# State space scan and maxout FFN on one core: where VectorE's scan steps stand among the Strassen products

## The chip, the core and the metric

One core of a Trainium2 chip runs the whole program: TensorE (PE) multiplies matrices, VectorE (DVE) and ScalarE (ACT) work element by element, GpSimd (POOL) too, and SyncE (SP) issues most transfers. Matrix results land in PSUM, eight banks of 512 float32 values on each of 128 partitions; the rest lies in SBUF. Each engine works through its instructions in the order in which the program lists them. The metric is the time of one execution on the device in microseconds (us), as the median of several runs.

## The reference

For each of 4 batches and 8 heads, over 768 tokens, a state space scan (chunks of 32 in the reference), and then a feed-forward layer on the heads side by side:

```python
y_intra = (C B^T * exp(cum_i - cum_j) * causal) x          # cum: running sum of log a
y_inter = exp(cum_i) * (C state)
state   = exp(sum log a) * state + sum_j exp(cum_last - cum_j) B_j x_j
h   = maximum(maximum(y @ w1, y @ w2), y @ w3)             # y: 3072 x 256, w: 256 x 768
out = h @ w_out                                            # 768 x 256
```

Everything is float32 in and out; head dimension 32, state dimension 16.

## The kernel before

The 768 tokens are cut into six blocks of 128, numbered 0 to 5; one block holds 128 tokens of all four batches, 512 columns. Block 0 is done first, with plain matmuls for the three weight matrices (`up`, line 559 of the new text, 554 of the old). Blocks 1 to 5 use Strassen's scheme with seven products instead of eight: for each of the three weight matrices and three pairs of column tiles there is one step k, 0 to 8, which the text below calls "product k" of its block. `early(c, k)` issues four matmuls, two into the bank `sumA` and two into `sumB`; ScalarE copies the first (`eu`, line 639), VectorE adds up `eu`, `v` and an early sum (lines 640 to 642). `late(c, k)` then adds three more matmuls onto the same banks, so TensorE must wait there until the early readings are done. VectorE reads the results in lines 655 and 656 and takes the maximum over the three weight matrices (lines 655 and 660). `sumA` has one bank, `sumB` two, `ffn` one; four banks, `att`, serve the scan in turn.

While block c goes through its nine products, the scan of block n = c + 1 is prepared between them. In product 0 the inputs B and C are transposed (`trB`, `trC`), ScalarE scales C (`CT`) and takes exp of E, and VectorE makes the scaled C, `Cd` (line 435), by reading the bank of `trC`. In products 1 and 3 `scores` issues eight matmuls each (line 476), into four `att` banks; of each four, the last one takes the bank that `trC`, or the fourth bank of the first four, held. VectorE multiplies each of the four banks by its decays, in place (`scan_weight`, line 484). In products 5 to 7 the output y of the scan is summed up (lines 501 and 514) and copied (line 522). `scan_sums` makes four differences of y (line 532), which the Strassen products of the next block use. `down_next` issues one half of an output tile of the projection (line 676) for an earlier block, as work for TensorE between the early and the late matmuls or behind them; the last half of a tile is copied and stored (line 682). A float32 matmul stands in the trace as two records.

The order on each engine is that in which the code emits instructions; nothing reorders it but this: VectorE's scan steps and the maximum are not emitted on the spot but put into the list `later`, and `pop(n)` emits the first n of them. Where the `pop` calls stand thus sets VectorE's order. The names k, c and n are those of the last loop.

Of the kernel before, what the change touches and what calls it, by code (L numbers as in the profile page):

```python
# [13 lines left out]
ALU = mybir.AluOpType  # L14
# [5 lines left out]
def kernel(  # L20
# [20 lines left out]
    nc = tc.nc  # L41
# [4 lines left out]
    NC = S // P  # L46
# [52 lines left out]
    a0 = const.tile([P, P], FP32, name="a0")  # L99
    for k in range(REP):  # L100
# [5 lines left out]
        out=a_sb,  # L106
# [15 lines left out]
    def load(c, name):  # L122
        src, w = sources[name]
        t = blocks[c][name] = raw.tile([P, BH, w], FP32, tag="raw_" + name, name="raw_" + name)
        nc.sync.dma_start(
            out=t, in_=src[:, :, c * P:(c + 1) * P, :].rearrange("b h s n -> s (b h) n"))
# [74 lines left out]
    def decode():  # L201
# [21 lines left out]
        out=pick, in_=ident.rearrange("p (r k) -> p k r", k=BH), op=ALU.add, axis=AX.X)  # L223
    npick = const.tile([P, BH], FP32, name="npick")
    nc.vector.tensor_scalar(
        out=npick, in0=pick, scalar1=-1.0, scalar2=None, op0=ALU.mult)
# [4 lines left out]
        out=hsel, in_=hsel, pattern=[[-N, NH]], compare_op=ALU.is_ge, fill=0.0,  # L231
        base=0, channel_multiplier=1)
    nc.gpsimd.affine_select(
        out=hsel, in_=hsel, pattern=[[N, NH]], compare_op=ALU.is_ge, fill=0.0,
# [3 lines left out]
        out=parity, in_=hsel.rearrange("p (r g) -> p g r", g=2), op=ALU.add, axis=AX.X)  # L238
# [6 lines left out]
        out=mask, in_=mask, pattern=[[1, P]], compare_op=ALU.is_ge, fill=MASKED,  # L245
# [119 lines left out]
    def decay_load(c):  # L365
        L = decays(c)
        for b in range(0, NB, 2):
            nc.sync.dma_start(
                out=L[:, b:b + 2].rearrange("j b h i -> j (b h) i"),
                in_=cums[b * NH:(b + 2) * NH, c, :].partition_broadcast(P))  # L370

    def last_load(c):
        E = blocks[c]["E"] = raw.tile([HN, NB, P], FP32, tag="E", name="E")
        rows = cums[:, c].rearrange("(b h) s -> h b s", h=NH)
        for h in range(NH):
            nc.sync.dma_start(out=E[h * N:(h + 1) * N], in_=rows[h].partition_broadcast(N))
# [41 lines left out]
    def scan_c(c):  # L418

        st = blocks[c]  # L420
        tr = st["trC"]
        st["CT"] = CT = att.tile([HN, NB, 2, P], FP32, tag="CT", name="CT")
        for g in range(2):
            nc.scalar.mul(CT[:, :, g], tr, parity[:, g:g + 1])

    def scan_e(c):
        E = blocks[c]["E"]
        nc.scalar.activation(E, E, AF.Exp)

    def scan_cd(c):  # L430

        st = blocks[c]
        E = st["E"]
        st["Cd"] = Cd = att.tile([HN, NB, P], FP32, tag="Cd", name="Cd")
        nc.vector.tensor_tensor(out=Cd, in0=st["trC"], in1=E, op=ALU.mult)
# [86 lines left out]
            nc.scalar.copy(out=yT[c][:, t], in_=blocks[c]["y"][t].rearrange("p b i -> p (b i)"))  # L522

    def scan_sums(c):
        y11, y12, y21, y22 = (
            yT[c][:, k, r * HB:(r + 1) * HB] for k in range(2) for r in range(2))
        late = [blocks[c]["y"][k].rearrange("p b i -> p (b i)")[:, r * HB:(r + 1) * HB]
                for k in range(2) for r in range(2)]
        t = ysum[c % 2]
        for k, (a1, a0) in enumerate((  # L530
                (late[1], y11), (late[3], t[:, 0]), (late[3], y12), (late[2], t[:, 1]))):
            nc.vector.tensor_tensor(out=t[:, k], in0=a1, in1=a0, op=ALU.subtract)  # L532
        sides[c] = {1: y11, 2: y21, 3: y22, 4: t[:, 3], 5: t[:, 0], 6: t[:, 1], 7: t[:, 2]}


# [7 lines left out]
    def h_of(c):  # L543
        if c not in hT:
            hT[c] = ffn.tile([P, NF, BLK], FP32, tag="h", name="h")
        return hT[c]
# [31 lines left out]
    NW = 3 * NQ  # L578
# [16 lines left out]
    def weight_sums(k):  # L595
        q, i = divmod(k, 3)
        a11, a12, a21, a22 = (
            w_sb[i][:, kk, (2 * q + g) * P:(2 * q + g + 1) * P]
            for g in range(2) for kk in range(2))
        s1, s2, s3, s4 = (wsum[k][:, j] for j in range(4))  # L600
        nc.gpsimd.tensor_tensor(out=s1, in0=a21, in1=a22, op=ALU.add)
        nc.gpsimd.tensor_tensor(out=s3, in0=a11, in1=a21, op=ALU.subtract)
        nc.gpsimd.tensor_tensor(out=s2, in0=s1, in1=a11, op=ALU.subtract)
        nc.gpsimd.tensor_tensor(out=s4, in0=a12, in1=s2, op=ALU.subtract)
# [9 lines left out]
    def products(c, k, which, first):  # L614
        for p, bank, half in which:
            nc.tensor.matmul(  # L616
                out=bank[:, half], lhsT=left(p, k), rhs=sides[c][p],
                start=(first and half == 0), stop=True, skip_group_check=True)

    later = []  # L620

    def pop(n):
        while n and later:
            later.pop(0)()
            n -= 1
# [19 lines left out]
    def late(c, k):  # L645
        q, i = divmod(k, 3)
        m = held["m"]
        A, B, eu, t = held.pop("open")
        products(c, k, [(2, A, 0), (3, B, 0), (4, B, 1)], False)
        to = h_of(c)[:, 2 * q:2 * q + 2].rearrange(  # L650
            "p g (r t) -> p (g r) t", r=2) if i == 2 else m
        if i == 0:
            nc.scalar.copy(out=m[:, 0], in_=A[:, 0])
        else:
            nc.vector.tensor_tensor(out=to[:, 0], in0=m[:, 0], in1=A[:, 0], op=ALU.max)
        nc.vector.tensor_tensor(  # L656
            out=t[:, 0:2], in0=B, in1=eu[:, 1:2].to_broadcast([P, 2, HB]), op=ALU.add)
        pop(1)
        if i > 0:
            later.insert(0, lambda: nc.vector.tensor_tensor(  # L660
                out=to[:, 1:4], in0=m[:, 1:4], in1=t, op=ALU.max))

    downs = []

    def down_next(kind=ffn_bank):

        if not downs:
            return
        c, j = downs.pop(0)
        u, i, half = j // 4, j // 2 % 2, j % 2  # L670
        if j % 4 == 0:
            held["o"] = kind([P, 2, DM], "o")
        o = held["o"]
        b = 2 * u + i
        for f in range(half * NQ, (half + 1) * NQ):
            nc.tensor.matmul(  # L676
                out=o[:, i], lhsT=hT[c][:, f, b * P:(b + 1) * P], rhs=wo_sb[:, f],
                start=(f == 0), stop=(f == NF - 1), skip_group_check=True)
        if j % 4 == 3:
            ob = ffn.tile([P, 2, DM], FP32, tag="ob", bufs=3, name="ob")  # L680
            nc.scalar.copy(out=ob, in_=o)
            nc.sync.dma_start(
                out=out.rearrange("(b s) m -> s b m", s=S)[c * P:(c + 1) * P, 2 * u:2 * u + 2],
                in_=ob)
# [34 lines left out]
    for _ in range(6):  # L719
# [4 lines left out]
        out=cums.rearrange("k c s -> (k c) s").rearrange("(w r) s -> r w s", w=2), in_=a_sb)  # L724
# [31 lines left out]
    def loads(c):  # L756
        if c < NC:
            decay_load(c)
            last_load(c)
            load(c, "B")  # L760
            load(c, "C")
            load(c, "x")
# [41 lines left out]
    scan_y(1)  # L804
    part(2)
    scan_sums(1)
    weight_sums(1)
    down_next()

    for c in range(1, NC):  # L810
        n = c + 1
        for k in range(NW):
            early(c, k)
            if k < 4:
                for _ in range((1, 2, 1, 1)[k] if c == 1 else min(k, 1)):
                    part(n)
            else:
                part(n + 1)
            pop(2)

            if n < NC and k in (0, 1, 3, 7):
                if k == 0:
                    transposed(n)
                elif k == 7:
                    scan_own(n, (2, 3))
                    scan_y(n)
                else:
                    scores(n, k - 1)
            elif n < NC or k < NW - 1:
                if c > 1 or k % 2 == 0:  # L830
                    down_next()
            late(c, k)

            if c == 1 and k + 2 < NW:
                weight_sums(k + 2)
            if n < NC:
                if k == 0:
                    loads(c + 2)
                    scan_c(n)
                    scan_e(n)  # L840
                    later.append(lambda: scan_cd(n))
                if k < 3 and c > 1:
                    down_next()
                elif k == 3 and n + 1 < NC:
                    decay_mask(n + 1, 0)
                elif k == 4 and n < NC - 1:
                    scan_state(n)
                elif k == 5:
                    scan_old(n)
                elif k == 6:  # L850
                    pop(9)
                    scan_own(n, (0, 1))
                elif k == 7:
                    scan_sums(n)
        pop(9)
        while downs:
            down_next()
        downs += [(c, j) for j in range(8)]
    while downs:
        down_next(att_bank)  # L860
# [30 lines left out]
```

## Time and profile before

| | us |
|---|---|
| median of 3 runs | 335.22 (333.2, 335.22, 335.3) |
| profiled execution | 333.45 |
| its span, first to last instruction | 331.7 |
| TensorE busy in it | 302.5 |
| VectorE busy in it | 200.4 |
| ScalarE busy in it | 120.2 |

The span is what the rows tell of; the execution's own time holds 1.75 us around it. Busy times of different engines overlap. Where a row ends in brackets, the first number is how long the engine was idle before it, and the name behind the arrow is what ended that idle time. Times in the rows are counted from the span's start.

### The profile page before, as it was taken

Reading aid. Unit: us, or ns where it says so; the run is one execution under the profiler, and the core shown is the slowest. Engines: PE = TensorE matmul, PEld = TensorE weight load, DVE = VectorE, ACT = ScalarE, POOL = GpSimd, SP = SyncE. Lnnn points to the kernel's source line nnn. Section 1 sums busy time; section 2 is a strip of 40 time slices with the busy share of each in tenths; the row PEclk is TensorE's granted clock in tenths of the full one; section 3 lists DMA queues with packets and bytes.
Section 4 is the critical chain, followed back from the end, with each engine's and each line's share of the span. In section 5 each row is a group of like instructions: output and inputs, shape, how many; then the busy total and the mean of one; then the engine's idle time right before and its main releaser. Section 6 shows DMA issues by size and latency. Waiting matters only on the chain.

```text
span 331.7 us, 5268 instructions
## 1 busy us (share of the span) xinstructions
PE 302.5 (91%) x2016; PEld 228.0 (69%) x2016; DVE 200.4 (60%) x384; ACT 120.2 (36%) x311; POOL 72.5 (22%) x94
## 2 busy tenths in 40 slices
PE   6779998898889988979999879999897999999995
PEld 4534443586666865858887667877686777888874
DVE  2697656824847584736656484658366658466540
ACT  2847468467321524222354232244431021110200
POOL 5133573699105610000600100500000000000000
PEclk9999999999979999978999997999999999999999
DMA  8997989987910198500007890001000000010001
GB/s 87 273 355 197 146 246 252 126 160 217 120 13 0 34 239 112 65 32 2 0 2 209 141 126 0 3 1 34 0 2 31 0 2 32 0 35 0 32 2 63
DMA packets 105017, 28.13 MB, mean 85 GB/s; under 512 B 75296, under 2 KB 101920, under 8 KB 104992
## 3 DMA queue, kind: packets, MB, share of 16 engines
q1 hardware_dynamic: 104688, 27.66, 40.6%
q8 instruction: 16, 0.26, 0.3%
q10 hardware_dynamic: 304, 0.13, 0.1%
q14 instruction: 9, 0.07, 0.1%
HBM read 24.54 MB, written 3.24 MB: 84 GB/s over the span
## 4 chain that ended last, share of the span: by engine, by line
PE 66%; DVE 18%; ACT 7%; issue 4%; POOL 3%; DVEq 0%; ACTq 0%; POOLq 0%
PE sumB L616 19%; PE o L676 17%; PE sumA L616 17%; PE s L476 3%; PE y L514 3%; ACT L L390 3%; DVE L L484 2%; DVE v L641 2%; DVE eu L640 2%; DVE rb L532 2%; PE y L501 2%; POOL w_u L185 1%; DVE h L660 1%; DVE rb L656 1%; DVE w_u L176 1%
## 5 line engine op out<-in xcount | busy, mean ns | idle before, releaser
L676 PE MATMUL o<-wo,h 128*128 128x256 f32 x288 | 69.4, 381 | 1.3 <-DVE wo L188 1.3
L676 PEld LDWEIGHTS o<-wo,h 128*128 128x128 f32 x288 | 54.3, 190 | 9.9 <-DVE wo L188 2.1
L616 PE MATMUL sumA<-yT,w 128*128 128x256 f32 x180 | 59.1, 411 | 1.6 <-DVE eu L640 0.9
L639 ACT COPY eu<-sumA 128x256 f32<-128x256 f32 x45 | 16.8, 373 | 119.6 <-PE sumA L616 101.1
L390 ACT ACTIVATE L<-L,ncums 128x128 f32<-128x128 f32 x160 | 50.9, 396 | 11.4 <-POOL L L379 11.4
L616 PE MATMUL sumB<-rb 128*128 128x256 f32 x180 | 46.5, 381 | 0.0
L640 DVE TENSOR_TENSOR eu<-sumA,eu 128x256 f32<-128x256 f32 x45 | 19.1, 424 | 38.4 <-ACT eu L639 38.4
L616 PEld LDWEIGHTS sumA<-yT,w 128*128 128x128 f32 x180 | 32.3, 196 | 14.4 <-issue 4.8
L616 PEld LDWEIGHTS sumB<-rb 128*128 128x128 f32 x180 | 34.7, 193 | 4.9
L476 PE MATMUL s<-CT,BT 32*128 32x256 f32 x192 | 21.4, 427 | 15.5 <-DVE L L484 7.7
L554 PE MATMUL up<-yT,w 128*128 128x512 f32 x72 | 32.3, 598 | 1.5 <-DVE w L188 1.5
L484 DVE TENSOR_TENSOR L<-s,L 128x512 f32<-128x512 f32 x48 | 31.3, 682 | 0.0
L616 PE MATMUL sumB<-yT,rb 128*128 128x256 f32 x90 | 29.0, 405 | 1.8 <-DVE rb L642 1.2
L379 POOL TENSOR_SCALAR_AFFINE_SELECT L<-L 128x1024 f32<-128x1024 f32 x20 | 23.6, 1188 | 28.2 <-DMA L<-cums 28.2
L476 PEld LDWEIGHTS s<-CT,BT 32*128 32x128 f32 x192 | 12.2, 188 | 24.2 <-DVE L L484 9.9
L616 PE MATMUL sumB<-rb,w 128*128 128x256 f32 x90 | 28.2, 396 | 0.0
L616 PE MATMUL sumA<-rb 128*128 128x256 f32 x90 | 27.5, 388 | 0.0
L656 DVE TENSOR_TENSOR m<-sumB,eu 128x512 f32<-128x512 f32 x15 | 10.4, 692 | 26.6 <-PE sumB L616 26.6
L554 PEld LDWEIGHTS up<-yT,w 128*128 128x128 f32 x72 | 13.2, 190 | 18.1 <-issue 12.6
L656 DVE TENSOR_TENSOR rb<-sumB,eu 128x512 f32<-128x512 f32 x30 | 20.7, 691 | 7.4 <-PE sumB L616 7.0
L185 POOL TENSOR_TENSOR w_u<-w_u,w_r 128x512 uint32<-128x512 uint32 x12 | 18.1, 1506 | 31.4 <-DVE w_u L179 30.3
L616 PEld LDWEIGHTS sumB<-yT,rb 128*128 128x128 f32 x90 | 17.1, 198 | 7.3 <-DVE rb L642 2.4
(93 smaller groups left out, 330.4 us busy)
## 6 DMA issues: line engine op xcount, KB each, us to landing
L<-cums SPq DMA_DIRECT2D x10, 1024.0 KB, 9.3
rb<-in_moe_w_dram SPq DMA_DIRECT2D x9, 512.0 KB, 8.6
raw_x<-in_x_dram SPq DMA_DIRECT2D x6, 512.0 KB, 7.6
out_dram<-ob SPq DMA_DIRECT2D x12, 256.0 KB, 2.1
raw_B<-in_B_dram SPq DMA_DIRECT2D x6, 256.0 KB, 4.2
raw_C<-in_C_dram SPq DMA_DIRECT2D x6, 256.0 KB, 6.4
rb<-in_moe_w_out_dram SPq DMA_DIRECT2D x3, 512.0 KB, 5.7
E<-cums SPq DMA_DIRECT2D x40, 32.0 KB, 4.0
```

Source lines behind the costliest of these rows:

```text
L185: nc.gpsimd.tensor_tensor(out=u, in0=u, in1=r, op=ALU.add)
L379: nc.gpsimd.affine_select(out=Ls[c][:, b], in_=Ls[c][:, b], pattern=[[0, NH], [1, P]], compare_op=ALU.is_ge, fill=MASKED, base=0, channel_ ...
L390: nc.scalar.activation(L[:, b, h], L[:, b, h], AF.Exp, bias=ncum[c][:, b * NH + h:b * NH + h + 1], scale=1.0)
L476: nc.tensor.matmul(out=banks[r][:, i].rearrange("j g i -> j (g i)"), lhsT=st["BT"][rows, b], rhs=st["CT"][rows, b].rearrange("p g i -> p ( ...
L484: nc.vector.tensor_tensor(out=M, in0=s, in1=M, op=ALU.mult)
L514: nc.tensor.matmul(out=st["y"][t][q * D:(q + 1) * D, b], lhsT=st["x"][:, b * NH + h], rhs=M[:, b, h], start=(c == 0 and b == 0), stop=True ...
L554: nc.tensor.matmul(out=p, lhsT=w_sb[i][:, k, f * P:(f + 1) * P], rhs=yT[c][:, k], start=(k == 0), stop=(k == KD - 1))
L616: nc.tensor.matmul(out=bank[:, half], lhsT=left(p, k), rhs=sides[c][p], start=(first and half == 0), stop=True, skip_group_check=True)
L639: nc.scalar.copy(out=eu[:, 0], in_=A[:, 0])
L640: nc.vector.tensor_tensor(out=eu[:, 1], in0=A[:, 1], in1=eu[:, 0], op=ALU.add)
L656: nc.vector.tensor_tensor(out=t[:, 0:2], in0=B, in1=eu[:, 1:2].to_broadcast([P, 2, HB]), op=ALU.add)
L676: nc.tensor.matmul(out=o[:, i], lhsT=hT[c][:, f, b * P:(b + 1) * P], rhs=wo_sb[:, f], start=(f == 0), stop=(f == NF - 1), skip_group_check ...
```

## The change

The change touches only when VectorE's steps are emitted, and the place of one piece of the projection.

- `scan_sums` emits only the first of the four differences of y at once and puts the other three at the head of `later`.
- `late` no longer emits a step of its own and returns the maximum to the caller, which puts it at the head of `later` behind another `pop`.
- In product 0 the loads, the scaling of C, exp of E come ahead of that `pop`, so that Cd is emitted at the end of product 0. In product 1 the `pop` takes two steps, and so two score weights.
- After the early part of product 8 four steps are emitted: the three differences and the maximum. The block's last maximum waits until the next block's product 0.
- In block 1 a piece of the projection stands in product 8 and not in product 4.

```diff
@@ scan_sums
-        for k, (a1, a0) in enumerate((
-                (late[1], y11), (late[3], t[:, 0]), (late[3], y12), (late[2], t[:, 1]))):
-            nc.vector.tensor_tensor(out=t[:, k], in0=a1, in1=a0, op=ALU.subtract)
+        steps = [
+            lambda k=k, a1=a1, a0=a0: nc.vector.tensor_tensor(
+                out=t[:, k], in0=a1, in1=a0, op=ALU.subtract)
+            for k, (a1, a0) in enumerate((
+                (late[1], y11), (late[3], t[:, 0]), (late[3], y12), (late[2], t[:, 1])))]
+        steps[0]()
+        later[:0] = steps[1:]
@@ late
-        pop(1)
         if i > 0:
-            later.insert(0, lambda: nc.vector.tensor_tensor(
-                out=to[:, 1:4], in0=m[:, 1:4], in1=t, op=ALU.max))
+            return [lambda: nc.vector.tensor_tensor(
+                out=to[:, 1:4], in0=m[:, 1:4], in1=t, op=ALU.max)]
+        return []
@@ the loop over blocks and products
     scan_sums(1)
+    pop(9)
     weight_sums(1)
...
-            pop(2)
+            pop(4 if k == NW - 1 else 2)
...
-                if c > 1 or k % 2 == 0:
+                if c > 1 or k in (2, 6, 8):
                     down_next()
-            late(c, k)
+            maximum = late(c, k)
 
             if c == 1 and k + 2 < NW:
                 weight_sums(k + 2)
+            if n < NC and k == 0:
+                loads(c + 2)
+                scan_c(n)
+                scan_e(n)
+                later.append(lambda: scan_cd(n))
+            pop(2 if k == 1 else 1)
+            later[:0] = maximum
             if n < NC:
-                if k == 0:
-                    loads(c + 2)
-                    scan_c(n)
-                    scan_e(n)
-                    later.append(lambda: scan_cd(n))
                 if k < 3 and c > 1:
                     down_next()
...
-        pop(9)
-        while downs:
-            down_next()
+        if n == NC:
+            pop(9)
         downs += [(c, j) for j in range(8)]
```

VectorE's order, block 1, from the end of product 0 into product 1; before:

```order
L656 TENSOR_TENSOR m<-sumB,eu 128x512
L640 TENSOR_TENSOR eu<-sumA,eu 128x256
L641 TENSOR_TENSOR v<-sumB,eu 128x256
L642 TENSOR_TENSOR rb<-sumB,v 128x256
L435 TENSOR_TENSOR Cd<-trC,E 128x512
L655 TENSOR_TENSOR m<-m,sumA 128x256
L656 TENSOR_TENSOR rb<-sumB,eu 128x512
L484 TENSOR_TENSOR L<-s,L 128x2x256
```

and now (lines 640 to 642, 655, 656 and 660 are 645 to 647, 660, 661 and 664 in the new text):

```order
L661 TENSOR_TENSOR m<-sumB,eu 128x512
L435 TENSOR_TENSOR Cd<-trC,E 128x512
L645 TENSOR_TENSOR eu<-sumA,eu 128x256
L646 TENSOR_TENSOR v<-sumB,eu 128x256
L647 TENSOR_TENSOR rb<-sumB,v 128x256
L660 TENSOR_TENSOR m<-m,sumA 128x256
L661 TENSOR_TENSOR rb<-sumB,eu 128x512
L484 TENSOR_TENSOR L<-s,L 128x2x256 x2
```

Cd moved ahead of the three early steps of product 1, and two score weights (`L<-s,L`) stand where one did. In product 3 of the same block, before:

```order
L640 TENSOR_TENSOR eu<-sumA,eu 128x256
L641 TENSOR_TENSOR v<-sumB,eu 128x256
L642 TENSOR_TENSOR m<-sumB,v 128x256
L660 TENSOR_TENSOR h<-m,rb 128x768
L484 TENSOR_TENSOR L<-s,L 128x2x256
L656 TENSOR_TENSOR m<-sumB,eu 128x512
```

and now:

```order
L645 TENSOR_TENSOR eu<-sumA,eu 128x256
L646 TENSOR_TENSOR v<-sumB,eu 128x256
L647 TENSOR_TENSOR m<-sumB,v 128x256
L664 TENSOR_TENSOR h<-m,rb 128x768
L661 TENSOR_TENSOR m<-sumB,eu 128x512
```

The fourth weight of the first four left product 3. At the end of a block, from the last step of product 7 through product 8, now:

```order
L661 TENSOR_TENSOR rb<-sumB,eu 128x512
L532 TENSOR_TENSOR rb<-y,yT 128x256
L645 TENSOR_TENSOR eu<-sumA,eu 128x256
L646 TENSOR_TENSOR v<-sumB,eu 128x256
L647 TENSOR_TENSOR rb<-sumB,v 128x256
L532 TENSOR_TENSOR rb<-y,rb 128x256
L532 TENSOR_TENSOR rb<-y,yT 128x256
L532 TENSOR_TENSOR rb<-y,rb 128x256
L664 TENSOR_TENSOR m<-m,rb 128x768
L660 TENSOR_TENSOR h<-m,sumA 128x256
```

Before, all four differences (line 532) stood in front of `eu`. The other blocks change in the same way. GpSimd's and SyncE's own orders stay as they were; TensorE's and ScalarE's change only by the moved piece of the projection and its copy.

## Rows read from the trace of the kernel before

**Rows 1.** Span and mean granted clock; busy us, share of the span, instructions.

```profile
core 0: 331.7 us, clock 0.979
...
PE 302.5 (91%) x2016; PEld 228.0 (69%) x2016; DVE 200.4 (60%) x384; ACT 120.2 (36%) x311; POOL 72.5 (22%) x94
```

**Rows 2.** TensorE's waits: line, releaser, us in total, times, longest.

```profile
PE s L476 <- DVE L L484: 7.7, 4, 1.9
PE s L476 <- DVE Cd L435: 4.9, 4, 1.3
```

**Rows 3.** Stretches: length, busy us by engine, granted clock (before the last two).

```profile
92.00:100.00 8.00, 7.43 (x32) 6.02 (x33) 3.43 (x7) 1.93 (x6) 0.00 (x0) 0.79 0.02 3
128.00:132.00 4.00, 2.81 (x22) 1.94 (x22) 1.91 (x4) 1.55 (x5) 0.00 (x0) 1.00 1.22 115
144.00:152.00 8.00, 6.89 (x22) 5.10 (x23) 2.35 (x4) 0.61 (x2) 0.00 (x0) 0.58 0.00 0
200.00:204.00 4.00, 4.00 (x12) 2.91 (x11) 0.57 (x1) 0.37 (x1) 0.00 (x0) 0.59 0.00 0
248.00:252.00 4.00, 2.08 (x20) 1.25 (x19) 2.74 (x5) 1.55 (x5) 0.00 (x0) 1.00 0.19 66
```

**Rows 4.** Timeline, block 3, products 0 and 1: start, length, engine, instruction.

```profile
181.04 0.64 ACT L428 ACTIVATE E<-E 128x512 f32<-128x512 f32 x1
...
183.15 0.42 DVE L640 TENSOR_TENSOR eu<-sumA,eu 128x256 f32<-128x256 f32 x1 [1.93 <-ACT eu L639]
...
184.14 0.42 DVE L642 TENSOR_TENSOR rb<-sumB,v 128x256 f32<-128x256 f32 x1
184.51 0.69 DVE L435 TENSOR_TENSOR Cd<-trC,E 128x512 f32<-128x512 f32 x1
...
185.35 1.10 PE L476 MATMUL s<-CT,BT 32*128 32x256 f32 x10 [1.20 <-DVE Cd L435]
...
186.91 0.59 PE L616 MATMUL sumB<-yT,rb 128*128 128x256 f32 x2
```

**Rows 5.** Timeline, block 3, products 2 and 3.

```profile
190.59 0.42 DVE L640 TENSOR_TENSOR eu<-sumA,eu 128x256 f32<-128x256 f32 x1 [1.33 <-ACT eu L639]
...
194.32 0.68 DVE L484 TENSOR_TENSOR L<-s,L 128x512 f32<-128x512 f32 x1
...
197.18 0.42 DVE L642 TENSOR_TENSOR m<-sumB,v 128x256 f32<-128x256 f32 x1
...
198.39 0.69 DVE L484 TENSOR_TENSOR L<-s,L 128x512 f32<-128x512 f32 x1
...
199.13 1.42 PE L476 MATMUL s<-CT,BT 32*128 32x256 f32 x10 [1.92 <-DVE L L484]
```

**Rows 6.** Timeline, block 3's start: product 8 of block 2, product 0 of block 3.

```profile
172.10 0.41 DVE L532 TENSOR_TENSOR rb<-y,yT 128x256 f32<-128x256 f32 x1
...
172.41 0.37 ACT L639 COPY eu<-sumA 128x256 f32<-128x256 f32 x1 [1.52 <-PE sumA L616]
...
176.28 0.30 PEld L616 LDWEIGHTS sumA<-yT,w 128*128 128x128 f32 x2 [0.47 <-DVE h L655]
```

**Rows 7.** Timeline, block 1, products 2 and 3.

```profile
84.75 0.42 DVE L640 TENSOR_TENSOR eu<-sumA,eu 128x256 f32<-128x256 f32 x1
...
88.02 0.70 PE L616 MATMUL sumA<-yT,w 128*128 128x256 f32 x2 [0.25 <-DVE h L655]
```

**Rows 8.** Costliest groups: the projection; busy us, mean ns, idle before.

```profile
L676 PE MATMUL o<-wo,h 128*128 128x256 f32 x288 | 69.4, 381 | 1.3 <-DVE wo L188 1.3
```

**Rows 9.** Timeline, block 1, product 4 and product 8.

```profile
99.22 0.42 DVE L642 TENSOR_TENSOR rb<-sumB,v 128x256 f32<-128x256 f32 x1
...
100.16 0.59 PE L616 MATMUL sumB<-yT,rb 128*128 128x256 f32 x2
...
119.61 0.70 PE L616 MATMUL sumA<-yT,w 128*128 128x256 f32 x2 [0.91 <-DVE eu L640]
```

**Rows 10.** Timeline of SyncE's queue, block 1.

```profile
115.59 0.37 SPq L368 DMA_DIRECT2D L<-cums  x1
```

## Prediction

> **What bounds the kernel now.** I read the share of each engine first, then who waits for whom on TensorE, then the granted clock by stretches, then the timeline at the places that the change touches. TensorE is busy 91% of the span and VectorE 60% [rows 1]: TensorE sets the time, and what can be won is its idle time and its lost clock. In its list of waits two lines stand out, both on the scores matmuls of line 476: 7.7 us in four waits of up to 1.9 us for the weighting of line 484, and 4.9 us in four waits of up to 1.3 us for Cd of line 435 [rows 2]. Both are VectorE work. The third loss is the clock. Its mean is 0.979 of 331.7 us [rows 1], so 7.0 us are lost, and 6.7 us of that lie in three stretches: 8 us at 0.79, 8 us at 0.58 and 4 us at 0.59, which lose 1.68, 3.36 and 1.64 us [rows 3]. At full clock TensorE runs at 2.4 GHz; in these stretches it runs in part at the other level, 1.2 GHz.
>
> The reader should see where the clock falls. Blocks 1, 2 and 3 each have one low stretch, and each follows the 1.92 us wait of product 3 (in block 3 the wait ends at 199.13 [rows 5] and the low window begins at 200). Block 4 has the same wait, TensorE busy only 2.08 us of 4 there, and keeps its clock [rows 3]. After the 1.2 us wait of product 1 the clock is full: the window 128:132 is one of four such places [rows 3]. So the longer wait brings the fall three times in four, the shorter one never.
>
> **Part 1: Cd in product 0.** Now VectorE does Cd behind eu, v and the last early sum of product 1, at 184.51, and the fourth scores bank, which the transposed C held until then, comes free at 185.2; TensorE goes on at 185.35 after 1.20 us [rows 4]. In the new order Cd stands ahead of eu. It waits for ScalarE's exp of E, which ends at 181.04 + 0.64 = 181.68. VectorE is idle for 1.93 us before eu at 183.15 [rows 4], so Cd's 0.69 us fit: it ends near 182.4, an estimate, and TensorE wants the bank at 185.35 - 1.20 = 184.15. What is queued behind the waiting Cd is eu, which waits longer anyway, for ScalarE's copy. What comes next on TensorE are the late products. Those in sumB stand at 186.91; they would start at 185.7 and need the early sum that ends at 184.14 + 0.42 = 184.56 [rows 4]. So nothing else is late, and the whole 4.9 us goes. Bounds: 0 if another reader holds the bank, 4.9.
>
> **Part 2: score weights in pairs.** Of the first four weightings, product 1 takes two and not one, and the fourth leaves product 3, where it ran at 198.39 and released TensorE at 199.13 [rows 5]. It now stands where the third stands, 194.32 + 0.68 = 195.0, over 1 us before the scores of product 3. The extra one in product 1 takes 0.68 us ahead of eu of product 2; there VectorE is idle for 1.33 us [rows 5], in blocks 2 to 4. Once the wait is gone the late products of product 3 come 1.92 us sooner and need the sum that ends at 197.60 [rows 5], long past by then. Gain 7.7 us; bounds 0 to 7.7.
> In block 1 there is no such cover: eu of product 2 follows the weighting at 84.75 with no idle time, and TensorE waits already 0.25 us for line 655 at 88.02 [rows 7]. There I count 0.6 us of cost, since neighbours on VectorE overlap a little (the sum that ends at 184.56 is followed by Cd at 184.51 [rows 4]); bounds 0 and 0.7.
>
> **Part 3: the clock.** Without the waits of product 3 I take the three low stretches as gone: 6.7 us; bounds 0 and 6.7, below nothing too if new gaps bring new falls (a rival). I take the upper end because the fall never follows the gaps of 1.2 us or less, and no wait as long as 1.9 us remains in these blocks. The Trainium skill (TensorE: Matmul & The Clock Gate, section HAM oscillation — how this bites in real kernels) shows the clock falling after waits on transfers between bursts of matmuls, and the waits in its example are longer than any here. By that rule the waits of product 3 would not be the cause, and the sum would be 321.9; the trace does not agree, since each of the three falls comes straight behind a wait of 1.92 us.
>
> **Part 4: the sums of y.** Three of the four go behind the last product's early sums, and the last maximum goes into the next block. What gates the next block is line 655 of product 8: it frees the only sumA bank, and TensorE waits 0.47 us for it at 176.28 [rows 6]. Ahead of line 655 stands the same VectorE work as before, only in another order, so this wait stays. The order adds a little: the first sum ends at 172.10 + 0.41 = 172.51, and behind it now comes eu, which must wait for ScalarE's copy to end at 172.41 + 0.37 = 172.78 [rows 6]. That is 0.27 us of idle time, less what the second sum no longer waits for the first; I take 0.2 us. Four boundaries: 0.8 us of cost; bounds 0 and 1.6. The deferred maximum lies in product 0 behind the early sums, where VectorE waits for TensorE's late products anyway; I cost it at nothing, and without that cover it would be its own length at each boundary.
>
> **Part 5: the projection moved in block 1**, from product 4 to product 8. In product 4 its cover goes: the late products in sumB, now at 100.16, could start sooner by its length (6 of 288 records that take 69.4 us: 1.45 us [rows 8]), but wait for the early sum that ends at 99.22 + 0.42 = 99.64 [rows 9], so only 0.4 us is won. In product 8 TensorE waits 0.91 us for eu and more behind it [rows 9]; the projection fills that and costs nothing, since line 655 still gates. Gain 0.4 us; bounds -1.0 (not hidden at all, 1.45 less 0.4) and 0.4. With it moves block 0's last store, and behind that in SyncE's queue stand the loads for block 4, issued from 115.59 on [rows 10]. They will go out some 5 us later, an estimate (the wait in product 8 ends at 119.61 [rows 9], and the projection and its copy follow), and are wanted a block later, so I cost that at nothing; without that cover it would be up to 5 us once.
>
> **Sum** against the profiled execution (333.45 us, span 331.7 [rows 1] and 1.75 around it): 333.45 - 4.9 - 7.7 - 6.7 + 0.6 + 0.8 - 0.4 = 315.2. The median of the runs is 335.22, that is 1.77 more, about one further low-clock stretch (block 1's costs 1.68), which would go with the others. So I give 315.2 for the median too; if the difference has another cause, 317.0.
>
> **Rivals.**
> - *The clock is not won back* (14%): the falls have another cause than the wait, since block 4 has the wait and no fall [rows 3], and the same three stretches turn up elsewhere. 315.2 + 6.7 = 321.9; with one or two short ones 316.9 to 318.5. Against it: no fall stands anywhere else in these blocks. The Trainium skill's example in part 3, with its longer waits, would speak for it.
> - *The wait of product 1 stays* (6%), since ScalarE's copies of the same bank or the exp of E release it later than I read: 315.2 + 4.9 = 320.1. Against it: both end at 181.68 or sooner.
> - *The wait of product 3 stays with its clock loss* (5%): the fourth weighting would wait on its decays and not on its turn: 315.2 + 7.7 + 6.7 = 329.6, a gain near what can just be told. Against it: the same weighting runs today with no idle time noted before it.
> - *VectorE's order is the bound, and it comes out slower* (5%): Cd (0.69), the extra weighting (0.68) and three sums (3 x 0.41) only delay eu, v and the early sum, and the late products wait for these in place of the waits removed. The waits and the clock loss stay, plus 4 x 2.6 us: 333.45 + 10.4 = 343.9. It decides where VectorE's idle time before eu is below 0.69 us in product 1 and 0.68 us in product 2. In blocks 2 to 4 these are 1.93 and 1.33 [rows 4, 5]; only block 1 is short [rows 7].
>
> **The numbers.** The forecast, 315.2, has 70%, with its own range 313 to 317.5 (the bounds of parts 4 and 5 and the 1.8 of the median). To hold 8 in 10 the range takes in most of the first two rivals: 312.8 to 321. About 1% is what a measurement of this kernel can tell from no change. Faster by more: the forecast, the first two rivals and some of the third, 92%; within 1%: 4%; slower: 4%.
>
> **What would show it.** Right: both lines of waits at line 476 are gone; Cd runs between the sum of product 0 and eu of product 1; scores stand as sixteen records in one run in products 1 and 3; the mean clock is 0.995 or more; block 4, at full clock already, shortens by 1.20 + 1.92 less 0.2, some 2.9 us; the wait for line 655 at the boundaries is 0.4 to 0.8 us. Wrong: a clock below 0.99, or TensorE waiting at line 616 for eu or the early sum by about what the scores waited.

## The result and the profile after

The changed kernel takes 308.87 us, the median of four runs (308.51 to 310.01), against 335.26 us before in the same comparison: a ratio of 0.922 with a 95% interval of 0.917 to 0.928. Run again beside the experiments it took 309.04 us, a ratio of 0.920 (0.917 to 0.922). The direction was right; 315.2 us was forecast with a range down to 312.8, so the gain was larger than the range allowed.

The span, clock and busy time of the changed kernel, in the columns of [rows 1]:

```profile
core 0: 306.7 us, clock 0.999
```

```profile
PE 287.5 (94%) x2016; PEld 220.6 (72%) x2016; DVE 199.5 (65%) x384; ACT 119.7 (39%) x311; POOL 72.4 (24%) x94
```

VectorE does the same work, 200.4 us before and 199.5 now; TensorE is busy 15.0 us less with as many instructions, and the lost clock went from 7.0 us to 0.3 us. TensorE's longest waits, in the columns of [rows 2]:

```profile
PE sumA L621 <- DVE h L660: 3.7, 5, 1.0
PE s L476 <- ACT CT L424: 2.9, 2, 1.5
PE spread L300 <- POOL mask L244: 2.5, 1, 2.5
```

Both lines of [rows 2] are gone; the two waits of line 476 that are left stand ahead of block 1. At the head is now the block boundary, line 660 (655 before). The timeline of block 3, which answers to [rows 4] and [rows 5]:

```profile
166.60 0.69 DVE L435 TENSOR_TENSOR Cd<-trC,E 128x512 f32<-128x512 f32 x1 [0.49 <-ACT E L428]
...
168.04 0.42 DVE L645 TENSOR_TENSOR eu<-sumA,eu 128x256 f32<-128x256 f32 x1 [0.75 <-ACT eu L644]
...
171.62 1.28 DVE L484 TENSOR_TENSOR L<-s,L 128x512 f32<-128x512 f32 x2
...
173.63 0.42 DVE L645 TENSOR_TENSOR eu<-sumA,eu 128x256 f32<-128x256 f32 x1 [0.73 <-ACT eu L644]
```

Cd ran in a gap in front of eu, and the pair of score weights in the gap in front of the next eu; VectorE still waits 0.75 and 0.73 us for ScalarE behind them, so in this block neither delayed anything.

Where the time went is seen from when each product starts on TensorE, that is, the distance from one `early` to the next. Before and after, in us, for the products that changed:

| product | block 1 | block 2 | block 3 | block 4 | sum of changes |
|---|---|---|---|---|---|
| 0 | 3.96, 3.97 | 5.81, 5.35 | 5.34, 5.35 | 5.35, 5.35 | -0.4 |
| 1 | 6.25, 4.62 | 7.44, 5.59 | 7.45, 5.59 | 7.44, 5.59 | -7.2 |
| 2 | 4.74, 5.25 | 5.61, 5.61 | 5.61, 5.61 | 5.61, 5.61 | +0.5 |
| 3 and 4 | 13.68, 9.10 | 15.23, 9.29 | 13.54, 9.29 | 11.42, 8.81 | -17.4 |
| 8 | 4.99, 5.17 | 4.99, 5.18 | 4.98, 5.46 | 4.98, 5.18 | +1.0 |

Products 5 to 7 and block 5 are as long as before, within 0.03 us each. The rest, 1.5 us, lies ahead of the blocks: block 1 starts at 73.07 before and at 71.53 here. In the second profile of the changed kernel it starts at 72.98, so that part is a difference between executions and not the change.

In block 1 product 1 won only 1.63 us. There Cd ends after the scores have started:

```profile
76.86 0.69 DVE L435 TENSOR_TENSOR Cd<-trC,E 128x512 f32<-128x512 f32 x1 [0.47 <-ACT E L428]
...
77.32 1.47 PE L476 MATMUL s<-CT,BT 32*128 32x256 f32 x16
...
78.72 0.70 PE L621 MATMUL sumA<-yT,w 128*128 128x256 f32 x2
```

The sixteen score records take 78.72 - 77.32 = 1.40 us to the next product, and 1.07 in the other blocks: a rest of the wait is left, 0.33 us, which the list does not show, since the records around it overlap it.

### The profile page after: what moved, and what is told of

Its sections match the earlier page's. It is cut to its first block, busy times and chain, and to the rows that moved or that the text cites. A ratio compares the mean times of both kernels' runs of the same rounds, so it can differ in the third digit from the quotient of the medians.

```text
span 306.7 us, 5262 instructions
## 1 busy us (share of the span) xinstructions
PE 287.5 (94%) x2016; PEld 220.6 (72%) x2016; DVE 199.5 (65%) x384; ACT 119.7 (39%) x311; POOL 72.4 (24%) x94
## 4 chain that ended last, share of the span: by engine, by line
PE 74%; DVE 13%; ACT 6%; POOL 3%; issue 3%; POOLq 0%; ACTq 0%; DVEq 0%
PE sumB L621 22%; PE sumA L621 20%; PE o L681 18%; PE y L514 3%; PE s L476 3%; ACT L L390 2%; DVE L L484 2%; PE up L559 2%; PE y L501 2%; POOL w_u L185 2%; DVE w_u L176 2%; DVE m L664 1%; DVE rb L532 1%; PE spread L316 1%; DVE v L646 1%
## 5 line engine op out<-in xcount | busy, mean ns | idle before, releaser
L621 PE MATMUL sumA<-yT,w 128*128 128x256 f32 x180 | 56.9, 398 | 4.0 <-DVE h L660 3.7
L621 PEld LDWEIGHTS sumA<-yT,w 128*128 128x128 f32 x180 | 31.1, 189 | 15.8 <-DVE h L660 5.7
L621 PE MATMUL sumB<-yT,rb 128*128 128x256 f32 x90 | 27.3, 385 | 1.0 <-DVE rb L647 1.0
L621 PE MATMUL sumA<-rb 128*128 128x256 f32 x90 | 26.8, 379 | 0.0
L621 PE MATMUL sumB<-rb,w 128*128 128x256 f32 x90 | 26.8, 379 | 0.0
L646 DVE TENSOR_TENSOR v<-sumB,eu 128x256 f32<-128x256 f32 x45 | 19.1, 425 | 4.7
L621 PEld LDWEIGHTS sumB<-yT,rb 128*128 128x128 f32 x90 | 16.4, 190 | 5.2 <-issue 2.0
L621 PEld LDWEIGHTS sumB<-rb,w 128*128 128x128 f32 x90 | 17.1, 190 | 2.3
L621 PEld LDWEIGHTS sumA<-rb 128*128 128x128 f32 x90 | 17.1, 190 | 2.4
```

What stands on the lines that cost most here:

```text
L621: nc.tensor.matmul(out=bank[:, half], lhsT=left(p, k), rhs=sides[c][p], start=(first and half == 0), stop=True, skip_group_check=True)
L646: nc.vector.tensor_tensor(out=v, in0=B[:, 1], in1=eu[:, 1], op=ALU.add)
```

## The wait was longer than its row

The forecast priced each wait of the scores by the idle time in the list. The rows of block 4, whose clock was full before and after, show what that misses. Before (start, length of the group, instructions):

```profile
248.83 0.71 PE L476 MATMUL s<-CT,BT 32*128 32x256 f32 x6
251.46 1.13 PE L476 MATMUL s<-CT,BT 32*128 32x256 f32 x10 [1.92 <-DVE L L484]
252.51 0.70 PE L616 MATMUL sumA<-yT,w 128*128 128x256 f32 x2
```

and the changed kernel, the same place:

```profile
226.24 1.15 PE L476 MATMUL s<-CT,BT 32*128 32x256 f32 x16
227.32 0.70 PE L621 MATMUL sumA<-yT,w 128*128 128x256 f32 x2
```

From the first score record to the next product it was 252.51 - 248.83 = 3.68 us, and is 227.32 - 226.24 = 1.08 us: the wait cost 2.60 us, not 1.92. The list counts idle time from the end of the row of six, 248.83 + 0.71 = 249.54. The other 0.68 us might be waiting that the list hides, or the cost of cutting a run of score matmuls in two. A run from the experiments below tells them apart. In it the same sixteen records are cut at the same place, but TensorE does other matmuls in between and never waits (block 3):

```profile
185.82 0.71 PE L478 MATMUL s<-CT,BT 32*128 32x256 f32 x6
186.46 2.86 PE L775 MATMUL o<-wo,h 128*128 128x256 f32 x12
189.24 1.12 PE L478 MATMUL s<-CT,BT 32*128 32x256 f32 x10
190.30 0.70 PE L618 MATMUL sumA<-yT,w 128*128 128x256 f32 x2
```

Six records take 186.46 - 185.82 = 0.64 us there and ten take 190.30 - 189.24 = 1.06, together 1.70, where sixteen in one run take 1.08. So 0.62 of the 0.68 us is the cost of the cut, with no waiting in it. The single records show how it comes about: a score matmul uses 32 of the 128 rows (`32*128`), and in the unbroken run four records at a time start within 0.02 us of each other, so sixteen records are four rounds. The six before the cut are two rounds of three, and the ten behind it are four rounds again: the matmul that was held back no longer runs beside its three neighbours. What is left is the row's end: the next matmul starts 0.64 us after the six begin, 0.07 us before the end that the trace gives them. For block 4 the wait thus is 1.92 + 0.07 us of idle time and 0.64 + 1.05 - 1.08 = 0.61 us for the cut, 2.60 in all. For product 1 of block 3 the same sum is 1.20 + 0.07 + (0.64 + 1.02 - 1.07) = 1.86, from [rows 4] and its neighbours:

```profile
183.44 0.71 PE L476 MATMUL s<-CT,BT 32*128 32x256 f32 x6
...
186.37 0.70 PE L616 MATMUL sumA<-yT,w 128*128 128x256 f32 x2
```

186.37 - 183.44 = 2.93 us against 1.07 now. The Trainium skill (Perfetto Trace Analysis, section Tensor Engine Instruction (MATMUL, LD_WEIGHTS)) says that TensorE's ends in a trace are computed and not observed. The trace agrees in that the next matmul starts before the given end, but only 0.07 us of the 0.68 lie there.

## Experiments

**Cd alone.** One line is added to the kernel before:

```diff
                     later.append(lambda: scan_cd(n))
+                    pop(1)
```

> The kernel before with Cd alone moved to the end of product 0; score weights, sums of y and the projection stay where they were. Theory (a wait costs what lies between the start of the scores and the start of the next products, less the 1.07 us that sixteen score records take in one run): product 1 shrinks by 1.6 to 1.86 us in each of blocks 1 to 4, 7.2 us in all. Rival (a wait costs the idle time that the list of waits shows): 4.9 us in all. Clock: if a fall follows the wait of product 3, which stays here, at least one low stretch remains right behind it, and the time is about 326 to 328 us; if the two waits of a block bring the fall only together, the clock is full and the time is near 321.

It took 322.32 us, a ratio of 0.964 (0.957 to 0.971). Product 1 went from 6.25, 7.44, 7.45 and 7.44 us to 4.63, 5.59, 5.59 and 5.59, 7.2 us in all; the size by starts is right and 4.9 is not. The waits of product 3 stood unchanged in the list:

```profile
PE s L476 <- DVE L L484: 7.7, 4, 1.9
```

The clock fell behind two of them, those of blocks 2 and 3 (columns as in [rows 3]; the waits end near 139 and at 189.5):

```profile
136.00:140.00 4.00, 2.08 (x19) 1.07 (x17) 2.74 (x5) 1.25 (x5) 0.00 (x0) 1.00 0.19 66
140.00:144.00 4.00, 4.00 (x11) 3.22 (x11) 0.93 (x2) 0.37 (x1) 0.00 (x0) 0.57 0.00 0
188.00:196.00 8.00, 6.47 (x27) 5.18 (x28) 3.57 (x7) 1.69 (x6) 0.00 (x0) 0.79 0.10 34
```

The time lies below the 326 to 328 us expected, because these two falls cost 1.72 and 1.68 us where before the three cost 6.7, and block 1 started 0.9 us earlier. So the place of the falls came as forecast here, and the time did not.

**Pairs alone.** The kernel before with

```diff
-        pop(1)
+        pop(2 if k == 1 else 1)
```

> The kernel before with two score weights in product 1 and the fourth in product 2, and nothing else; Cd stays in product 1, so its wait stays. Theory: product 3 shrinks at full clock from 6.9 us to 4.3 in each of four blocks, 10.4 us, product 2 of block 1 grows by 0.5, and the clock is full in all blocks, another 6.5: about 317 us. Rival on the size: 7.7 us and the clock, about 319.5. Rival on the clock (the fall does not hang on the wait of product 3): low stretches stay somewhere, about 323.5.

It took 316.37 us, 0.946 (0.938 to 0.954). Product 3 took 4.40, 4.30, 4.30 and 4.30 us, product 2 of block 1 went from 4.74 to 5.26, and every block kept full clock although the wait of product 1 stood as before:

```profile
PE s L476 <- DVE Cd L435: 4.9, 4, 1.3
```

So the clock's part hangs on the wait of product 3 and not on that of product 1, and the size by starts holds for it too: 333.45 - 10.4 - 6.7 + 0.5 = 316.9.

**The wait filled instead of removed.** To the kernel with Cd alone, in product 3 of blocks 2 to 4, between the third and the fourth score matmul:

```diff
+    def cover():
+        o = ffn_bank([P, 2, DM], "o")
+        for f in range(NF):
+            nc.tensor.matmul(
+                out=o[:, f % 2], lhsT=hT[n - 2][:, f, 0:P], rhs=wo_sb[:, f],
+                start=(f == 0), stop=(f == NF - 1), skip_group_check=True)
```

> The kernel with Cd alone moved, and in product 3 of blocks 2 to 4 six more matmuls of the projection's shape (2.6 us), whose sums nobody reads, issued between the third and the fourth score matmul, where TensorE otherwise waits for the score weight. The wait is not shortened, only filled. Theory (the idle time brings the fall): blocks 2 to 4 keep full clock behind product 3, product 3 takes the same 6.9 us as it did in block 4 at full clock, and the time is that of the kernel with Cd alone less the falls of blocks 2 and 3, some 5 us; block 1, not filled, may keep its fall. Rival (the place or the score matmuls bring the fall): falls in blocks 2 and 3 as before, the time no shorter.

It took 321.11 us, against 322.32 for the kernel without the filling; the two profiles' spans are 319.1 and 320.3. Both blocks kept full clock around product 3:

```profile
132.00:148.00 16.00, 16.00 (x110) 12.81 (x109) 10.92 (x21) 4.05 (x12) 0.00 (x0) 1.00 0.06 18
180.00:196.00 16.00, 16.00 (x82) 12.88 (x80) 10.85 (x21) 5.10 (x16) 0.00 (x0) 1.00 0.57 73
```

Product 3 took 7.7 us and not the 6.9 expected: the six matmuls take 189.24 - 186.46 = 2.78 us where the idle time was 1.99, and the cut in the scores costs as much as before. That eats 2.4 us, and only the two falls, 3.4 us, were there to win; so the 5 us expected were too many. For the cause it speaks plainly in one direction: in blocks 2 and 3 the clock fell in both profiles with the idle wait and in neither block with the wait filled. The mean clock of all their executions bears it out: 0.979 to 0.989 in the four with Cd alone, 0.997 to 0.999 in the four with the filling, 1.000 in the four with the pairs. It is not a proof for every wait, since blocks 1 (here and with Cd alone) and 4 have the idle wait and kept their clock; what decides between them the runs do not show.

**The boundary as it was.** The changed kernel with the four differences of y in one piece and the last maximum at the block's end:

```diff
-        steps[0]()
-        later[:0] = steps[1:]
+        for step in steps:
+            step()
...
-            pop(4 if k == NW - 1 else 2)
+            pop(2)
...
-        if n == NC:
-            pop(9)
+        pop(9)
```

> The changed kernel with the four differences of y in one piece behind product 7 again, and the block's last maximum at the block's end. Theory (the same VectorE work gates line 660 of the new text in either order, and the new order adds 0.2 us of idle time): product 8 goes from 5.2 us back to 5.0 in each of four blocks, and where GpSimd works beside the last maximum (block 1's end) product 0 of block 2 may grow by 0.4; 308 to 309 us, 0 to 0.8 shorter. Rival (the sums behind the early steps were worth something): 1 us or more longer.

308.45 us against 309.04 for the changed kernel beside it:

> The changed kernel once more, as the measure for the other kernels that run beside it: about 309 us, mean clock 0.995 or more, each block's products as in its first profile.

Product 8 took 4.98 to 4.99 us in all four blocks, against 5.17, 5.18, 5.45 and 5.18. So this part of the change costs 1.0 us by the traces; the medians differ by 0.6, within the spread of the runs. Product 0 of block 2 did not grow by the 0.4 us that I had allowed for; it took 5.36 us, as in the changed kernel.

**Line 660 first.** From [rows 6] and the wait at the head of the new list: what stands in front of line 660 in product 8 but is not needed yet goes behind it.

```diff
-            pop(4 if k == NW - 1 else 2)
+            pop(2)
...
-            later[:0] = maximum
+            if n < NC and k == NW - 1:
+                later.extend(maximum)
+            else:
+                later[:0] = maximum
```

> The changed kernel, but in product 8 only two of the three remaining differences of y go ahead of line 660's reading of sumA; the fourth comes behind it, and the maximum of product 7 waits for the next block's product 0 along with the last one. Theory (this reading gates the next block's first product; 0.34 + 0.87 us of VectorE work leaves its front, TensorE idles there 0.70 to 0.98 us): product 8 shrinks by 0.7 to 1.0 us in four blocks, 3 to 4 us in all, 305 to 306 us. Rival (the two maxima in product 0 delay its late readings and move the wait there): product 0 grows by as much, no gain.

It took 305.17 us, a ratio of 0.908 to the kernel before (0.906 to 0.910), 3.9 us below the changed kernel. Product 8 of block 2 in the changed kernel, and then in this one:

```profile
159.84 0.95 DVE L664 TENSOR_TENSOR m<-m,rb 128x768 f32<-128x768 f32 x1
...
160.71 0.41 DVE L660 TENSOR_TENSOR h<-m,sumA 128x256 f32<-128x256 f32 x1
...
161.17 0.70 PE L621 MATMUL sumA<-yT,w 128*128 128x256 f32 x2 [0.70 <-DVE h L660]
```

```profile
160.16 0.42 DVE L660 TENSOR_TENSOR h<-m,sumA 128x256 f32<-128x256 f32 x1
160.39 0.59 PE L621 MATMUL sumB<-rb,w 128*128 128x256 f32 x2
160.82 0.59 PE L621 MATMUL sumA<-yT,w 128*128 128x256 f32 x2
```

Without the maximum in front, line 660 follows TensorE's late product, and the next block starts right behind the late ones. Product 8 took 4.31 or 4.32 us in every block, 0.86 to 1.14 less, and product 0 did not grow (5.24 to 5.29 in blocks 2 to 4), so nothing moved there.

**And in product 2.** On top of that:

```diff
-            pop(2)
+            pop(1 if n < NC and k == 2 else 2)
...
-            pop(2 if k == 1 else 1)
+            pop(2 if k in (1, 2) else 1)
```

> As the kernel before it in this list, and in product 2 the third score weight goes behind line 660's reading of sumA too, with the fourth. Theory: in block 1 product 2 goes from 5.25 us back to 4.7, elsewhere nothing changes, since TensorE does not wait there; 0.5 us less than the kernel before it. Rival: the fourth weight comes too late for the scores of product 3, and a wait of 0.3 us or more shows there in four blocks; slower by 1 us or more.

304.09 us, 0.905 (0.903 to 0.908), the fastest kernel here. Product 2 of block 1 went from 5.26 to 4.66 us; product 3 stayed at 4.29 to 4.43 us. By the traces this is worth 0.6 us; the rest of the 1.1 us between the medians may be the spread of the starts (block 1 starts at 72.25 in this profile and at 73.00 in the other).

## Why the prediction was wrong, step by step

- *What bounds the kernel*: right. TensorE's waits at line 476 and its clock were what could be won, and they made 24.3 of the 25.0 us that the span lost: 7.2 + 10.4 + 6.7.
- *Part 1 (Cd), the step that failed first*: the mechanism was right, and the term was mis-sized. "The whole 4.9 us goes" was the list's idle time; the kernel with Cd alone won 7.2 us there. What the term left out is 0.66 us at each wait, nearly all of it the cut in the run of scores, less the 0.33 that stayed in block 1. The upper bound was set at the same 4.9, so the range could not hold it.
- *Part 2 (pairs)*: the same fault, 7.7 us put down where four times 2.60, 10.4 us, lay. The sign on record for block 4, some 2.9 us shorter, shows both terms at once: it is 4.3 us shorter. The 0.6 us of cost in block 1 was 0.5.
- *Part 3 (the clock)*: 6.7 us forecast and 6.7 measured: products 3 and 4 lost 17.4 us, less 10.4 for the waits and 0.3 for the projection. Falls came behind idle waits of 1.92 us, and none came where these were gone or filled. The Trainium skill (TensorE: Matmul & The Clock Gate, section HAM oscillation — how this bites in real kernels) has longer waits in its example than these. The weighing against it came out for the rows.
- *Part 4 (the sums)*: 0.8 us of cost forecast, 1.0 measured. But the wait for line 660 did not just stay. At the end of block 2 the last product's late matmuls started 0.45 us late for the early sums before and are on time now, while the next block's start came 0.23 us late and comes 0.86 us late now (distances between starts, less the 0.43 us that such a pair of records takes in an unbroken run): 0.68 against 0.86, the 0.2 us of cost, in another place. That it could be removed by a third order, I did not see.
- *Part 5 (the projection)*: 0.4 us won was forecast. Product 4 of block 1 took 4.99 us at full clock with it and 4.70 without, 0.3 won, and product 8 took it up for nothing. The later loads behind it were forecast to cost nothing; they won 0.5 us, as the last point shows.
- *The median*: taken to be one more low stretch in the runs than in the profile. That the clock makes the difference is borne out by the later runs of the kernel before: the ten beside the last experiments have spans of 330.8 and 331.3 us at a mean clock of 0.979 and of 333.6 to 335.5 at 0.962 to 0.969; of the seven beside the first, one of 331.5 us at 0.972 fits less well. How many stretches it is, no trace of those runs shows.
- *Not foreseen*: product 0 of block 2 became 0.5 us shorter. Before, the last maximum ran there beside GpSimd's mask and took 1.41 us where it takes 0.95 alone:

```profile
122.07 1.09 POOL L379 TENSOR_SCALAR_AFFINE_SELECT L<-L 128x1024 f32<-128x1024 f32 x1 [9.16 <-DMA L<-cums]
122.56 1.41 DVE L660 TENSOR_TENSOR h<-m,rb 128x768 f32<-128x768 f32 x1
123.89 0.41 DVE L640 TENSOR_TENSOR eu<-sumA,eu 128x256 f32<-128x256 f32 x1
```

The eu behind it was late, and with it the late products. The mask starts when its load has come (line 368), and in the changed kernel that load stands behind block 0's last store, which the moved projection brought to the end of block 1: the mask starts 5.8 us after block 2 begins and not 0.3. So it is the moved load that won this, and not the new place of the maximum: with the maximum back at the block's end (the boundary as it was) it took 0.96 us and product 0 5.36. The runs without the moved projection fit: the mask and the maximum overlap by 0.60, 0.61, 0.45 and 0.25 us in the kernel before, with Cd alone, with the wait filled and with the pairs, the maximum takes 1.41, 1.42, 1.27 and 1.06, and product 0 takes 5.81, 5.82, 5.66 and 5.46.

With the two terms by starts the forecast's own sum would have been 333.45 - 7.2 - 10.4 - 6.7 + 0.6 + 0.8 - 0.4 = 310.15; the earlier start of block 1 (1.5, which is luck and not the change) and the mask out of the way (0.5), less 0.2 for the boundary, give 308.35, where the profiled execution took 308.51. Of the rivals none came: the clock was won back, neither wait stayed but for 0.33 us in block 1, and VectorE's order did not become the bound. What was left out was a case on the other side, in which the waits are worth more than their rows.

## What to carry to other kernels

Price a wait inside a run of matmuls by the distance between starts on both sides of it, less what the same matmuls take in an unbroken run elsewhere in the trace; the idle time in a list of waits is a lower bound, not an upper one. Where the matmuls of such a run go side by side, a wait in their midst costs the rounds that the cut adds as well, and filling the wait with other work does not win these back; only an unbroken run does. In an in-order engine that frees buffers, put the reading that frees the scarcest buffer first and work that nobody waits for behind it; here that order took 3.9 us off the changed kernel, whose own order had lost 1.0 of them. Where the clock falls behind a wait, count the clock with the wait.

## What was not expected of the hardware

- A wait that interrupts eight score matmuls cost 0.66 to 0.68 us more than its idle time: 1.86 us for 1.20, and 2.60 for 1.92. Cut at the same place with no wait, the run cost 0.62 us more than unbroken.
- Behind a wait of 1.92 us the granted clock fell in three of four blocks before and in two of four with Cd alone, and never behind the eight waits of 1.19 to 1.30 us (before and with the pairs alone); each fall cost 1.6 to 3.4 us.
- A maximum on VectorE with both inputs in SBUF took 1.41 us beside GpSimd's mask, 0.95 without.
